# One query token against a sliding window: attention in units of two key-value pairs instead of one

## The chip, the cores and the metric

The kernel runs on one core of a Trainium2 chip. The metric is device time in microseconds for one execution. The profile of one execution shows the core's engines: TensorE (PE: matrix products into PSUM, the accumulators; PEld is its loading of weights), VectorE (DVE), ScalarE (ACT), GpSimd (POOL) and SyncE (SP), which here only issues transfers. 16 DMA engines bring data from HBM into SBUF, the on-chip memory of 128 partitions.

## What is computed

Two sequences (B = 2) decode one token each. `x` (2 x 512) is normalised to `xn`. Branch A is attention of 32 query heads over 8 key-value heads, four queries to one key-value head, over the last 4096 of 32768 cached positions. Branch B is a small gated perceptron. The end is `x + A * silu(B)`. All is float32.

```python
q = (xn @ wq).reshape(B, Sq, Hq, Dh).transpose(0, 2, 1, 3)     # 32 heads of 128
k = repeat(k_cache[:, :, Sk - W:, :], 4, axis=1)               # W = 4096
v = repeat(v_cache[:, :, Sk - W:, :], 4, axis=1)
p = softmax(einsum("bhqd,bhkd->bhqk", q, k) * Dh ** -0.5)
s = einsum("bhqk,bhkd->bhqd", p, v) ... @ wo
z = gelu(xn @ w_in); z1 = z[..., :Fh]; z2 = layernorm(z[..., Fh:])
g = silu((z1 * (w_sp * z2 + b_sp)) @ w_out)
return x + s * g
```

There are 2 x 8 = 16 pairs of a sequence and a key-value head. Each has 2 MiB of keys and 2 MiB of values to read: 64 MiB. The weights are wq (8 MiB), wo (8 MiB), w_in (3.5 MiB) and w_out (1.75 MiB).

## The kernel before

**Memory.** A pool `ring` (line 75) has four slots of 32 KB a partition. They hold, in turn, w_in, the two halves of wq, then one pair's keys and values together (`slot` in `load`, lines 114 to 120), at last the two halves of wo (lines 502 to 511). A slot is free when all that reads it is done. Position p*32 + j of a pair's window lies in partition p at place j, so that a partition reads 16 KB without a break from each cache. All large transfers are issued by SP, in the order of the program; SP waits at an issue until its slot is free, and every later issue waits behind it. `kts`, two buffers of 8 KB a partition (tag "kts" in the pool `sb`), holds transposed keys; `z`, `qs` and `qx` of the start share its buffers. `wout` has a place of its own (line 92).

**Start** (lines 87 to 322). `xn` is made and transposed. TensorE makes w_in's products `z` and transposes them (`zT_ps`), then the queries `q_ps` in four calls of `queries(k)` (lines 230 to 237), among them the perceptron's steps, then its second product `y`. The queries are copied (`qs`, ScalarE), transposed (`qx`, VectorE), spread (`xm`, `qa`) and placed by `place_queries` in `qb`, each in its own 32 columns. A few small constant matrices of zeros and ones (`sums`, `joint`, `heads`, `diag`, `selw`, `perm8`, `perm16`, lines 135 to 199) later do sums and rearrangements as matrix products.

**One pair**, functions of lines 340 to 436:

- `turn(p, q)`, q = 0 to 3: VectorE transposes a quarter of the keys (128 x 1024) in blocks of 32 x 32 into `kts`.
- `shares(p, r)`, r = 0, 1: four products of TensorE, side by side in the four column groups, multiply the queries with a quarter of the dimensions each; `keep` copies the 128 x 512 result with ScalarE and `scores` adds the four shares, with `sums` as weights. The scores of both halves of the window stand in one bank, 128 x 512.
- `row_max`, `spread_max`, `share_max`, `bias`: the maximum of each row, then over the partitions by a small product (`mo`), then the bias of the exponential.
- `probs`: ScalarE's exponential with a row sum; `probs_t`: VectorE transposes the result (128 x 512).
- `share_sum`, `weights`: the sum over partitions and its reciprocal.
- `pv(p, r)`: eight value products with 16 columns of weights and 512 values each, accumulated in `acc`; `evacuate`: four ScalarE copies scaled by the weights; `collect`: four products (`col`) bring the heads into order, and for the last pair of a set `gather` reduces them. The sets (line 327) are heads 0 to 3, 4 to 5 and 6 to 7 of both sequences.

**Order** (lines 462 to 495). One loop over the pairs, written out by hand, interleaves the turns, shares and scores of the current pair with the softmax and values of the one before and the collection of the one before that. Every engine runs its instructions in just this order (`InOrder`, line 26).

**End** (lines 525 to 570). After the last pair's softmax and values `spread` and `place` bring each set's outputs into `oT`. `wo_early` multiplies 24 of wo's 32 tiles into one bank `part`, in groups of four; the last eight, those of the third set, go into `so` together with the copied `part`. wo comes in pieces of 2, 2, 1, 1, 1, 0.5, 0.25 and 0.25 MiB, so that little is left to compute behind the last one. Two VectorE steps (`res`) apply the gate and add `x`, and SP writes 4 KB out.

Line numbers in the profile: nearly every instruction is issued by the helper of line 36, so that L36 is nearly all; the names of the tiles tell the steps apart.

Of the kernel before, what the change touches and what calls it, by code (L numbers as in the profile page):

```python
# [14 lines left out]
P = 128  # L15
# [5 lines left out]
def free_ap(t, offset, dims):  # L21

    return bass.AP(tensor=t.tensor, offset=t.offset + offset, ap=[list(t.ap[0])] + [list(d) for d in dims])

# [17 lines left out]
def kernel(  # L42
# [28 lines left out]
    SCALE = DH ** -0.5  # L71

    fit = ctx.enter_context(tc.tile_pool(name="fit", bufs=1))
# [13 lines left out]
    xs = sb.tile([B, D], F32, tag="o", name="xs")  # L87
# [4 lines left out]
    wout = cst.tile([P, FT, D], F32, tag="wout", name="wout")  # L92
# [16 lines left out]

    NP = B * HKV  # L110

    slots = {}
# [22 lines left out]
    sums = cst.tile([P, G, REP, NR, 4], F32, tag="sums", name="sums")  # L135
# [16 lines left out]
    acc = [ps.tile([P, 4, DH], F32, tag=f"acc{a}", name=f"acc{a}") for a in range(2)]  # L152
    for a in range(2):
        dve.memset(acc[a], 0.0)

# [9 lines left out]
    xn = sb.tile([B, D], F32, tag="o", name="xn")  # L165
# [9 lines left out]
    for r in range(NR):  # L175
        dve.tensor_copy(sums[:, :, :, r, 0], rowm[:, 16 * r : 16 * r + 16].rearrange("p (g i) -> p g i", g=G))
    rm = cst.tile([P, G, NR], F32, tag="rm", name="rm")
    dve.tensor_reduce(
        rm, ident.rearrange("p (g i r x) -> p g r i x", g=G, r=NR, x=4)[:, :, :, :, 0], axis=AX.X, op=ALU.add
    )  # L180
    head = cst.tile([P, REP], F32, tag="head", name="head")
    dve.tensor_reduce(head, free_ap(rowm, 0, [[8, REP], [4, NR]]), axis=AX.X, op=ALU.add)
    heads = cst.tile([P, 32, REP], F32, tag="heads", name="heads")
    dve.tensor_copy(heads, free_ap(head, 0, [[0, 32], [1, REP]]))
    joint = cst.tile([P, G, REP, NR, 4], F32, tag="joint", name="joint")
    nc.gpsimd.memset(joint, 0.0)
    for r in range(NR):
        dve.tensor_copy(joint[:, :, :, r, 0], free_ap(head, 0, [[0, G], [1, REP]]))
    diag = cst.tile([P, 4], F32, tag="diag", name="diag")
    dve.tensor_reduce(diag, free_ap(rowm, 0, [[4, 4], [1, REP]]), axis=AX.X, op=ALU.add)  # L190
    dve.tensor_reduce(selw[:, 28:32], free_ap(rowm, 0, [[1, REP], [4, 4]]), axis=AX.X, op=ALU.add)
# [12 lines left out]
    z = sb.tile([P, F], F32, tag="kts", name="z")  # L204
# [23 lines left out]
    pq = [ps.tile([P, 512], F32, tag="s", name=f"q_ps{r}", bufs=2) for r in range(NR)]  # L228
# [57 lines left out]
    qs = sb.tile([P, NR, 512], F32, tag="kts", name="qs")  # L286
    qx = sb.tile([P, NR, HC, 32], F32, tag="kts", name="qx")
# [37 lines left out]
    JH = NT // NR  # L325
# [11 lines left out]
    class Pair:  # L337
# [12 lines left out]
    def shares(p, r):  # L350
        if r == 0:
            p.sh = bank(f"sh{p.n}", 512)
        for c in range(G):
            at = 32 * (G * p.n + c) + 16 * (1 - r)
            pe.matmul(
                p.sh[32 * c : 32 * c + 32, :], qb[:, at : at + 32], p.kt[r][:, :, 32 * c : 32 * c + 32],
                start=(r == 0), stop=(r == NR - 1),
            )

    def keep(p):  # L360
        p.ss = sb.tile([P, 512], F32, tag="ss", name=f"ss{p.n}")
        act.activation(p.ss, p.sh, AF.Copy)

    def scores(p):
        p.s = ps.tile([P, 512], F32, tag="s", name=f"s{p.n}", bufs=2)
        pe.matmul(p.s, sums.rearrange("p g i r x -> p (g i r x)"), p.ss, start=True, stop=True)

    def row_max(p):
        p.m = sb.tile([P, 1], F32, tag="m", name=f"m{p.n}")
        dve.reduce_max(p.m, p.s, axis=AX.X)  # L370

    def spread_max(p):
        p.mg = sb.tile([P, G * NR], F32, tag="mg", name=f"mg{p.n}")
        dve.tensor_scalar_mul(p.mg, rm.rearrange("p g r -> p (g r)"), p.m)

    def share_max(p):
        p.mo = ps.tile([P, 512], F32, tag="mo", name=f"mo{p.n}")
        pe.matmul(p.mo[:, : G * NR], joint.rearrange("p g i r x -> p (g i r x)"), p.mg, start=True, stop=True)

    def bias(p):  # L380
        p.nb = sb.tile([P, 1], F32, tag="nb", name=f"nb{p.n}")
        dve.reduce_max(p.nb, p.mo[:, : G * NR], axis=AX.X)
        dve.tensor_scalar_mul(p.nb, p.nb, -SCALE)

    def probs(p):
        p.p = sb.tile([P, JH, 32], F32, tag="p", name=f"p{p.n}")
        p.l = sb.tile([P, 1], F32, tag="l", name=f"l{p.n}")
        act.activation(
            p.p.rearrange("p j k -> p (j k)"), p.s, AF.Exp, bias=p.nb, scale=SCALE, accum_out=p.l,
        )  # L390

    def probs_t(p):
        p.pT = sb.tile([P, JH, 32], F32, tag="pT", name=f"pT{p.n}")
        dve.transpose(p.pT.rearrange("p j h -> p (j h)"), p.p.rearrange("p j k -> p (j k)"))

    def share_sum(p):
        pe.matmul(p.mo[:, 32:33], heads.rearrange("p a h -> p (a h)"), p.l, start=True, stop=True)

    def weights(p):
        w = sb.tile([P, 1], F32, tag="w", name=f"w{p.n}")  # L400
        dve.reciprocal(w, p.mo[:, 32:33])
        p.w = sb.tile([P, 4], F32, tag="wd", name=f"wd{p.n}")
        dve.tensor_scalar_mul(p.w, diag, w)

    def pv(p, r):
        for g in range(G):
            c = JH * r + 4 * g
            pe.matmul(
                acc[p.n % 2][32 * g : 32 * g + 4 * REP].rearrange("p a d -> p (a d)"),
                free_ap(p.pT, 32 * 4 * g + 4 * r, [[8, 4 * REP]]),  # L410
                p.v[:, c : c + 4, :].rearrange("p j d -> p (j d)"), start=(r == 0), stop=(r == NR - 1),
            )

    def evacuate(p):
        p.o = sb.tile([P, 4, DH], F32, tag="o", name=f"o{p.n}")
        for jj in range(4):
            act.activation(p.o[:, jj, :], acc[p.n % 2][:, jj, :], AF.Copy, scale=p.w[:, jj : jj + 1])

    col = {}

    def collect(p):
        b, kv = divmod(p.n, HKV)
        a0, n, o1 = sets[kv]
        if a0 == 0:
            col[b] = ps.tile([P, 4, 32], F32, tag="col", name=f"col{p.n}")
        for a in range(4):
            pe.matmul(
                col[b][32 * a : 32 * a + 32], selw[:, 28 - REP * a0 : 60 - REP * a0], p.o[:, :, 32 * a : 32 * a + 32],
                start=(a0 == 0), stop=(a0 == n - 1),
            )  # L430

    def gather(p):
        b, kv = divmod(p.n, HKV)
        a0, n, o1 = sets[kv]
        if a0 == n - 1:
            dve.reduce_sum(o1[:, b, :], col[b].rearrange("p a j -> p j a"), axis=AX.X)

    def spread(i):
# [3 lines left out]
        pt = bank(f"oT_ps{i}", B, nj)  # L442
        for x in range(nx):
            pe.matmul(
                pt, perm[:, x].rearrange("p h a x -> p (h a x)"), o1[:, :, nj * x : nj * x + nj],
                start=(x == 0), stop=(x == nx - 1),
            )
        return pt

    def place(i, pt):  # L450
        dve.tensor_copy(sets[f"oT{i}"][1][:, :, 0 : 16 * B : 16], pt.rearrange("p b j -> p j b"))

    def do(f, p, *a):
        if p is not None:
            f(p, *a)

    pairs = []
    for n in range(NP):
        p = Pair()
        p.n, p.kt = n, {}  # L460
        pairs.append(p)
    AHEAD = 6
    old = prev = None
    for cur in pairs:
        if cur.n <= AHEAD:
            cur.k = load(cur.n, 0)
        if AHEAD <= cur.n < NP - 1:
            pairs[cur.n + 1].k = load(cur.n + 1, 0)
        cur.v = load(cur.n, 1)
        do(turn, cur, 0)  # L470
        if cur.n == 0:
            place_queries()
        do(row_max, prev)
        do(turn, cur, 1)
        do(shares, cur, 0)
        do(spread_max, prev)
        do(share_max, prev)
        do(collect, old)
        do(turn, cur, 2)
        do(turn, cur, 3)  # L480
        do(bias, prev)
        do(probs, prev)
        do(probs_t, prev)
        do(shares, cur, 1)
# [114 lines left out]
```

## Time and profile before

| | |
|---|---|
| median of 3 runs | 218.5 us (218.18 to 219.12) |
| the profiled execution | 219.69 us |
| its span, from the first to the last instruction | 217.6 us |
| mean granted clock of TensorE | 0.84 |
| VectorE, ScalarE busy | 123.7 us, 49.6 us |
| bytes read from HBM | 89.4 MB |

How to read the lines: a row of a group has the operation, output <- inputs with shapes, the count, then after the first bar the busy time in us and the mean ns of one, and after the second the idle time of the engine ahead of it with what ended it. One float32 product is two MATMUL instructions. In the timeline a row starts with its start and its length in us. A row of the table by stretches has the stretch, its length, the busy time of PE, PEld, DVE, ACT and POOL with the number of instructions, the granted clock of TensorE (1.00 is full), the share of DMA time and GB/s. In the 40 slices a digit is the busy share in tenths. The chain that ended last is followed back from the last instruction to what released each step.

### The profile page before, as it was taken

The numbers are of one execution on the slowest core, as the hardware profiler recorded it, in microseconds if no ns is written. First come the engines' busy times: TensorE is split into PE (matmuls) and PEld (weight loads), VectorE is DVE, ScalarE is ACT, GpSimd is POOL, SyncE is SP. The second block draws the span as 40 slices with busy tenths as digits, with TensorE's granted clock in tenths as the row PEclk, the third lists the DMA queues.
The fourth block names the chain that finished last, engine by engine and source line by source line (L and its number), as shares of the span: only waits on it lengthen the run. The fifth ranks groups of instructions, "written<-read, shape, count | busy, mean of one in ns | idle before, by whom it ended". The sixth has DMA issues, their size and how long they took to land.

```text
span 217.6 us, 2755 instructions
## 1 busy us (share of the span) xinstructions
PE 156.4 (72%) x1068; PEld 53.3 (24%) x1068; DVE 123.7 (57%) x249; ACT 49.6 (23%) x128; POOL 5.2 (2%) x19
## 2 busy tenths in 40 slices
PE   0189694946888089986898856767588856898993
PEld 0129420500222022221222211212122211225242
DVE  4511212583784677888789585866749485722001
ACT  4110211201122211433233233132222323113200
POOL 8000000000000000000000000000000000000000
PEclk9999587665599955999889999699958999558598
DMA  7999899999999999999999999999999999999970
GB/s 254 422 434 482 386 428 429 434 434 428 434 419 431 431 434 431 425 434 429 434 431 434 428 431 428 426 434 434 434 425 434 428 434 425 434 428 425 423 303 2
DMA packets 6524, 89.57 MB, mean 412 GB/s; under 512 B 734, under 2 KB 750, under 8 KB 1136
## 3 DMA queue, kind: packets, MB, share of 16 engines
q1 hardware_dynamic: 6492, 89.40, 96.4%
q8 instruction: 8, 0.13, 0.2%
q14 instruction: 4, 0.03, 0.0%
q10 hardware_dynamic: 20, 0.01, 0.0%
HBM read 89.40 MB, written 0.00 MB: 411 GB/s over the span
## 4 chain that ended last, share of the span: by engine, by line
DMA 52%; PE 28%; DVE 14%; ACT 3%; issue 1%; SPq 0%; ACTq 0%
DMA kv<-in_A_k_cache_dram 41%; DMA wq<-in_A_wq_dram 11%; DVE kts L36 11%; PE acc L36 9%; PE sh L36 6%; PE s L36 5%; PE part L36 3%; PE q_ps L36 2%; ACT ss L36 2%; DVE m L36 2%; PE oT_ps L36 1%; ACT o L36 1%; PE so L36 1%; PE col L36 1%; DVE gate L36 1%
## 5 line engine op out<-in xcount | busy, mean ns | idle before, releaser
L36 DVE STREAM_TRANSPOSE kts<-kv 128x1024 f32<-128x1024 f32 x64 | 77.2, 1227 | 16.9 <-DMA kv<-in_A_k_cache_dram 16.9
L36 PE MATMUL sh<-kts,qb 128*32 128x512 f32 x256 | 42.8, 746 | 32.6 <-DVE mg L36 24.7
L36 PE MATMUL acc<-kv,pT 128*16 128x512 f32 x256 | 36.1, 687 | 0.0
L36 ACT ACTIVATE o<-acc,wd 128x128 f32<-128x128 f32 x64 | 18.2, 367 | 60.1 <-PE acc L36 52.2
L36 PE MATMUL s<-ss,sums 128*128 128x512 f32 x32 | 22.7, 797 | 6.4 <-ACT ss L36 6.4
L36 ACT ACTIVATE p<-s,nb 128x512 f32<-128x512 f32 x16 | 11.0, 688 | 47.5 <-DVE nb L36 47.5
L36 DVE STREAM_TRANSPOSE pT<-p 128x512 f32<-128x512 f32 x16 | 11.4, 711 | 14.7 <-ACT p L36 14.7
L36 PEld LDWEIGHTS sh<-kts,qb 128*32 128x32 f32 x256 | 6.6, 121 | 51.5 <-issue 36.6
L36 PE MATMUL q_ps<-wq,xnT 128*32 128x512 f32 x64 | 10.8, 810 | 5.3 <-DMA wq<-in_A_wq_dram 5.3
L36 PEld LDWEIGHTS acc<-kv,pT 128*16 128x16 f32 x256 | 6.9, 117 | 27.6 <-issue 18.5
L36 DVE TENSOR_REDUCE m<-s 128x1 f32<-128x512 f32 x16 | 10.6, 662 | 4.3 <-PE s L36 4.3
L36 ACT ACTIVATE ss<-sh 128x512 f32<-128x512 f32 x16 | 9.6, 597 | 14.1 <-PE sh L36 12.7
L36 PEld LDWEIGHTS mo<-l,heads 128*128 128x128 f32 x32 | 5.6, 220 | 17.4 <-ACT p L36 17.4
L36 PEld LDWEIGHTS mo<-mg,joint 128*128 128x128 f32 x32 | 5.6, 219 | 16.7 <-issue 16.7
L36 PE MATMUL col<-o,selw 128*32 128x128 f32 x128 | 7.7, 319 | 1.3 <-ACT o L36 1.0
L36 PEld LDWEIGHTS s<-ss,sums 128*128 128x128 f32 x32 | 5.7, 224 | 9.4 <-ACT ss L36 6.9
L36 PE MATMUL z<-win,xnT 128*32 128x448 f32 x32 | 4.9, 752 | 3.8 <-DMA win<-in_B_w_in_dram 3.8
L36 PE MATMUL mo<-l,heads 128*128 128x1 f32 x32 | 6.9, 285 | 0.4
L36 PE MATMUL mo<-mg,joint 128*128 128x8 f32 x32 | 7.0, 293 | 0.0
L36 PE MATMUL zT_ps<-rowm,z 128*128 128x2 f32 x28 | 6.6, 370 | 0.0
L36 PEld LDWEIGHTS zT_ps<-rowm,z 128*128 128x128 f32 x28 | 6.5, 325 | 0.0
L36 PE MATMUL part<-wo,oT 128*32 128x512 f32 x48 | 6.4, 672 | 0.0
(107 smaller groups left out, 79.3 us busy)
## 6 DMA issues: line engine op xcount, KB each, us to landing
kv<-in_A_k_cache_dram SPq DMA_DIRECT2D x16, 2048.0 KB, 17.2
kv<-in_A_v_cache_dram SPq DMA_DIRECT2D x16, 2048.0 KB, 21.7
wq<-in_A_wq_dram SPq DMA_DIRECT2D x1, 4096.0 KB, 24.0
wq<-in_A_wq_dram SPq DMA_DIRECT2D x2, 2048.0 KB, 28.4
wo<-in_A_wo_dram SPq DMA_DIRECT2D x2, 2048.0 KB
win<-in_B_w_in_dram SPq DMA_DIRECT2D x1, 3584.0 KB
wo<-in_A_wo_dram SPq DMA_DIRECT2D x3, 1024.0 KB, 25.4
wout<-in_B_w_out_dram SPq DMA_DIRECT2D x1, 1792.0 KB, 14.8
```

What stands on the lines that cost most here:

```text
L36: return self.tc.keep_in_program_order(call(*args, **kwargs))
```

## The change

A **unit** is two neighbouring pairs of one sequence, interleaved over the partitions: even partitions hold the first pair, odd ones the second, each 64 consecutive positions (32 KB without a break). Keys and values of a unit are loads of 4 MiB with a ring slot each, so that 8 + 8 issues take the place of 16 + 16. The orders of the issues and of all steps are now read from a written list, `ORDER`, one word a step, with its unit and part behind the colon: K and V are the loads, T a turn, X and Y two of wo's tiles in `wo_early`.

- `turn` has 8 steps a unit, of the same size. `kts` is a pool of its own with two buffers of 16 KB; `wout`, `z`, `qs` and `qx` use these buffers too.
- `shares(p, a)` takes half of the unit's places and, for each of the two pairs i, every second column of the transposed keys; there are as many products as before. `s` has one bank for each half a; `keep`, `scores` and `row_max` are done for each half, as often as before in all.
- `spread_max`, `share_max`, `bias`, `share_sum`, `weights`, `evacuate`, `collect` are done once a unit: half as often. `other` puts a large offset into the bias of the rows of the other pair, so that their exponentials are zero.
- `probs` makes two exponentials for each half, one for each pair, and writes each to every second column of `p` (128 x 1024); `probs_t` transposes 128 x 1024. `own_sum` adds the four row sums.
- `pv` has the same number of products, with 32 columns of weights for 16. `acc` is no longer cleared at the start.
- wo is loaded by `load_wo` from the list; `wo_early` takes two tiles a step instead of four, and its steps stand among those of the last unit. The late part behind it is the same.

The lines that matter, cut:

```diff
+ORDER = """
+K:0 K:1 V:0 T:0.0 q:0 T:0.1 T:0.2 T:0.3 shares:0.0 T:0.4 T:0.5 T:0.6 keep:0.0 scores:0.0 T:0.7 shares:0.1 keep:0.1
+scores:0.1 rowmax:0.0
+K:2 V:1 T:1.0 T:1.1 T:1.2 rowmax:0.1 mg:0 shmax:0 T:1.3 silu:0 bias:0 shares:1.0 T:1.4 exp:0.0 probs_t:0.0 T:1.5 T:1.6
+exp:0.1 keep:1.0 pv:0.0 lsum:0 shsum:0 scores:1.0 T:1.7 shares:1.1 probs_t:0.1 pv:0.1 weights:0 keep:1.1 scores:1.1
+evac:0 col:0 rowmax:1.0
+K:3 V:2 T:2.0 T:2.1 T:2.2 rowmax:1.1 mg:1 shmax:1 T:2.3 bias:1 shares:2.0 T:2.4 exp:1.0 probs_t:1.0 T:2.5 T:2.6 exp:1.1
+keep:2.0 pv:1.0 lsum:1 shsum:1 scores:2.0 T:2.7 shares:2.1 probs_t:1.1 pv:1.1 weights:1 keep:2.1 scores:2.1 evac:1
+col:1 rowmax:2.0
...
+K:7 V:6 T:6.0 rowmax:5.1 T:6.1 mg:5 T:6.2 shmax:5 T:6.3 T:6.4 bias:5 exp:5.0 exp:5.1 T:6.5 shares:6.0 probs_t:5.0
+pv:5.0 lsum:5 T:6.6 keep:6.0 probs_t:5.1 T:6.7 shsum:5 scores:6.0 weights:5 shares:6.1 rowmax:6.0 pv:5.1
+V:7 T:7.0 wo:0 keep:6.1 evac:5 scores:6.1 col:5 T:7.1 T:7.2 rowmax:6.1 mg:6 shmax:6 gather:5 spread:0 T:7.3 bias:6
+T:7.4 T:7.5 shares:7.0 exp:6.0 probs_t:6.0 T:7.6 keep:7.0 pv:6.0 T:7.7 wo:1 exp:6.1 scores:7.0 shares:7.1 probs_t:6.1
+keep:7.1 lsum:6 shsum:6 scores:7.1 rowmax:7.0 weights:6 pv:6.1 evac:6 rowmax:7.1 mg:7 shmax:7 col:6 oT:0 bias:7
+gather:6 spread:1 exp:7.1 exp:7.0 probs_t:7.1 lsum:7 X:0.1 probs_t:7.0 X:0.3 X:0.2 shsum:7 weights:7 X:0.0 pv:7.0
+pv:7.1 oT:1 evac:7 X:0.7 Y:0.1 X:0.4 X:0.5 col:7 Y:0.0 X:0.6 gather:7 spread:2 oT:2 Y:0.3 Y:0.2
+"""
 
...
     ring = ctx.enter_context(tc.tile_pool(name="ring", bufs=4))
+    kts = ctx.enter_context(tc.tile_pool(name="kts", bufs=2))
...
+    wout = kts.tile([P, FT, D], F32, tag="kts", name="wout")
     sp.dma_start(wout, w_out.rearrange("(p j) d -> p j d", p=P))
     wq_v = wq.rearrange("(p k) f -> p k f", p=P)
...
-
-    def load(n, i):
-        b, kv = divmod(n, HKV)
-        if i == 0:
-            slots[n] = slot(f"kv{n}", 2, NT, DH)
-        src = (k_cache, v_cache)[i]
-        sp.dma_start(slots[n][:, i], src[b, kv, SK - W :, :].rearrange("(p j) d -> p j d", p=P))
-        return slots[n][:, i]
+    NU = NP // 2
+    UJ = 2 * NT
+
+    def load(u, src, name):
+        t = slot(f"{name}{u}", UJ, DH)
+        b, v = divmod(u, HKV // 2)
+        first = src[b, 2 * v, SK - W, :]
+        of = bass.AP(tensor=src.tensor, offset=first.offset, ap=[[UJ * DH, P // 2], [SK * DH, 2], [1, UJ * DH]])
+        sp.dma_start(t.rearrange("p j d -> p (j d)"), of)
+        return t
...
+    for i in range(2):
+        dve.tensor_copy(joint[:, :, :, i, 0], free_ap(rowm, 4 * i, [[0, G], [8, REP]]))
+    other = cst.tile([P, 2], F32, tag="other", name="other")
...
-    qs = sb.tile([P, NR, 512], F32, tag="kts", name="qs")
-    qx = sb.tile([P, NR, HC, 32], F32, tag="kts", name="qx")
+    qs = kts.tile([P, NR, 512], F32, tag="kts", name="qs")
+    qx = kts.tile([P, NR, HC, 32], F32, tag="kts", name="qx")
...
     def turn(p, q):
-        r, a = divmod(q, 2)
-        if a == 0:
-            p.kt[r] = sb.tile([P, JH, P], F32, tag="kts", name=f"kts{p.n}_{r}")
-        n = JH // 2
+        a, r = divmod(q, 4)
+        if r == 0:
+            p.kt[a] = kts.tile([P, JH, P], F32, tag="kts", name=f"kts{p.u}_{a}")
+        n = JH // 4
         dve.transpose(
-            p.kt[r][:, n * a : n * a + n].rearrange("p j d -> p (j d)"),
+            p.kt[a][:, n * r : n * r + n].rearrange("p j d -> p (j d)"),
             p.k[:, n * q : n * q + n].rearrange("p j d -> p (j d)"),
         )
...
+    def shares(p, a):
+        p.sh[a] = bank(f"sh{p.u}_{a}", 512)
+        for i in range(2):
+            for c in range(G):
+                at = 32 * (G * (2 * p.u + i) + c) + 16 * (1 - i)
+                pe.matmul(
+                    p.sh[a][32 * c : 32 * c + 32, :], qb[:, at : at + 32],
+                    free_ap(p.kt[a], 32 * c + i, [[P, JH], [2, 16]]), start=(i == 0), stop=(i == 1),
+                )
+
+    def keep(p, a):
+        p.ss[a] = sb.tile([P, 512], F32, tag="ss", name=f"ss{p.u}_{a}", bufs=1)
+        act.activation(p.ss[a], p.sh[a], AF.Copy)
+
+    def scores(p, a):
+        p.s[a] = ps.tile([P, 512], F32, tag=f"s{a}", name=f"s{p.u}_{a}")
+        pe.matmul(p.s[a], sums.rearrange("p g h i x -> p (g h i x)"), p.ss[a], start=True, stop=True)
...
+    def bias(p):
+        nb = sb.tile([P, 1], F32, tag="nb", name=f"nb{p.u}")
+        dve.reduce_max(nb, p.mo[:, : G * 4], axis=AX.X)
+        p.nb = sb.tile([P, 2], F32, tag="nb2", name=f"nb2_{p.u}")
+        dve.tensor_scalar(p.nb, other, nb, -SCALE, op0=ALU.add, op1=ALU.mult)
+        p.l = sb.tile([P, 2, 2], F32, tag="l", name=f"l{p.u}")
+
+    def probs(p, a):
+        p.p[a] = sb.tile([P, JH, 32], F32, tag="p", name=f"p{p.u}_{a}")
+        for i in range(2):
+            act.activation(
+                free_ap(p.p[a], i, [[2, 512]]), p.s[a], AF.Exp, bias=p.nb[:, i : i + 1], scale=SCALE,
+                accum_out=p.l[:, a, i : i + 1],
+            )
+
+    def probs_t(p, a):
+        p.pT[a] = sb.tile([P, JH, 32], F32, tag="pT", name=f"pT{p.u}_{a}")
+        dve.transpose(p.pT[a].rearrange("p j c -> p (j c)"), p.p[a].rearrange("p j k -> p (j k)"))
...
+    def pv(p, a):
+        if a == 0:
+            p.acc = ps.tile([P, 4, DH], F32, tag="acc", name=f"acc{p.u}", bufs=2)
+        for n in range(JH // 4):
+            g, c = n % G, JH * a + 4 * n
             pe.matmul(
-                p.sh[32 * c : 32 * c + 32, :], qb[:, at : at + 32], p.kt[r][:, :, 32 * c : 32 * c + 32],
-                start=(r == 0), stop=(r == NR - 1),
+                p.acc[32 * g : 32 * g + 32].rearrange("p a d -> p (a d)"),
+                free_ap(p.pT[a], 32 * 4 * n, [[4, 32]]), p.v[:, c : c + 4, :].rearrange("p j d -> p (j d)"),
+                start=(a == 0 and n < G), stop=(a == 1 and n >= JH // 4 - G),
             )
...
+    def load_wo(n):
+        t = slot(f"wo{n}", 16, D)
         a = 0
-        for i in of:
-            nj = SETS[i][2]
+        for i in ((0,), (1, 2))[n]:
             for j, n in (((0, 8), (8, 8)), ((0, 4), (4, 4)), ((0, 4), (4, 2), (6, 1), (7, 1)))[i]:
                 sp.dma_start(t[:, a : a + n, :], wo_s[i][:, j : j + n, :])
                 blocks.append((t[:, a : a + n, :], sets[f"oT{i}"][1], j))
                 a += n
+
     EARLY = 24
...
-    def wo_early(n, a0=0):
+    def wo_early(n, at):
         nonlocal done
+        if done == 0:
+            part.append(ps.tile([P, 512], F32, tag="s0", name="part"))
         t, oT, j = blocks[n]
-        for a in range(a0, a0 + 4):
+        for a in range(at, at + 2):
             g = done % G
             pe.matmul(
-                part[32 * g : 32 * g + 32, :], oT[:, j + a, :], t[:, a, :], start=(done < G), stop=(done >= EARLY - G)
+                part[0][32 * g : 32 * g + 32, :], oT[:, j + a, :], t[:, a, :], start=(done < G), stop=(done >= EARLY - G)
             )
             done += 1
 
...
+    for line in ORDER.strip().split("\n"):
+        for name in line.split():
+            name, at = name.split(":")
+            u, _, a = at.partition(".")
+            step(name, int(u), (int(a),) if a else ())
```

More of the change, by code (lines that the diff above doesn't have):

```diff
@@ L227 @@
     assert HKV == NR * G
-    pq = [ps.tile([P, 512], F32, tag="s", name=f"q_ps{r}", bufs=2) for r in range(NR)]
+    pq = [ps.tile([P, 512], F32, tag=f"s{r}", name=f"q_ps{r}") for r in range(NR)]
     def queries(k):
@@ L396, in share_sum @@
[L396 to L411, printed above, removed]
+    def shares(p, a):
+        p.sh[a] = bank(f"sh{p.u}_{a}", 512)
+        for i in range(2):
+            for c in range(G):
[4 more added lines that the diff above has]
+                )
@@ L545 @@
-    place(2, spread(2))
-    wo_early(0, 4)
-    wo_early(2)
-    wo_early(1, 0)
-    wo_early(1, 4)
-    wo_early(3)
-    parts = sb.tile([P, D], F32, tag="o", name="parts")
-    act.activation(parts, part, AF.Copy)
+    part = []
+    STEPS = dict(
+        T=turn, rowmax=row_max, mg=spread_max, shmax=share_max, bias=bias, exp=probs, probs_t=probs_t, lsum=own_sum,
+        shsum=share_sum, weights=weights, shares=shares, keep=keep, scores=scores, pv=pv, evac=evacuate, col=collect,
+        gather=gather,
+    )
```

233 lines of the change are left out of this document (97 added, 136 removed).

## The prediction

> **What bounds the kernel now.** First the top of the page and its 40 slices.
>
> ```profile
> span 217.6 us, 2755 instructions
> ...
> PE 156.4 (72%) x1068; PEld 53.3 (24%) x1068; DVE 123.7 (57%) x249; ACT 49.6 (23%) x128; POOL 5.2 (2%) x19
> ...
> DMA  7999899999999999999999999999999999999970
> GB/s 254 422 434 482 386 428 429 434 434 428 434 419 431 431 434 431 425 434 429 434 431 434 428 431 428 426 434 434 434 425 434 428 434 425 434 428 425 423 303 2
> ```
>
> No engine is busy for more than 72% of the span, while the DMA digits stand at 9 nearly everywhere up to the 38th slice. A slice is 217.6 / 40 = 5.44 us; the last two move 303 and 2 GB/s, so something goes on after the transfers. The table by stretches gives the rate and the end of the transfers (last two columns: DMA share, GB/s):
>
> ```profile
> 16.00:34.00 18.00, 15.32 (x90) 8.83 (x82) 3.56 (x18) 3.65 (x6) 0.00 (x0) 0.81 0.99 424
> 40.00:190.00 150.00, 110.65 (x742) 32.59 (x734) 107.87 (x179) 37.65 (x104) 0.00 (x0) 0.85 1.01 430
> 200.00:210.00 10.00, 9.59 (x66) 3.28 (x70) 1.06 (x6) 1.14 (x4) 0.00 (x0) 0.70 1.00 418
> 211.40:211.60 0.20, 0.20 (x8) 0.08 (x4) 0.00 (x0) 0.00 (x0) 0.00 (x0) 1.00 0.25 92
> ```
>
> 430 GB/s for 150 us, whatever the engines do, and the last bytes move at about 211.6. The kernel is a row of transfers with a tail of computing behind it. I read the tail in the timeline: TensorE's rows, VectorE's end, and the issues of the last two pieces of wo with their time to landing.
>
> ```profile
> 199.81 0.56 PE L36 MATMUL mo<-l,heads 128*128 128x1 f32 x2
> 200.30 3.62 PE L36 MATMUL acc<-kv,pT 128*16 128x512 f32 x16
> 203.70 1.93 PE L36 MATMUL part<-wo,oT 128*32 128x512 f32 x8
> 205.40 0.65 PE L36 MATMUL col<-o,selw 128*32 128x128 f32 x8
> 206.47 1.07 PE L36 MATMUL oT_ps<-o,perm 128*128 128x16 f32 x8 [0.41 <-DVE o L36]
> 207.46 4.50 PE L36 MATMUL part<-wo,oT 128*32 128x512 f32 x40
> 211.78 1.06 PE L36 MATMUL so<-wo,oT 128*32 128x128 f32 x32
> 212.74 0.43 PE L36 MATMUL so<-parts,rowm 128*32 128x128 f32 x8
> 212.98 1.06 PE L36 MATMUL so<-wo,oT 128*32 128x128 f32 x32
> ```
> ```profile
> 214.10 0.29 DVE L36 TENSOR_TENSOR res<-so,gate 128x128 f32<-128x128 f32 x1 [6.28 <-PE so L36]
> ```
> ```profile
> 187.59 5.17 SPq L36 DMA_DIRECT2D wo<-in_A_wo_dram  x2
> ```
> ```profile
> wo<-in_A_wo_dram SPq DMA_DIRECT2D x2, 256.0 KB, 23.8
> ```
>
> The first lands 23.8 us after 187.59, at 211.4; the second, issued long before that, stands behind it in the same queue: 0.26 MB / 430 GB/s = 0.6 us later, 212.0. TensorE, though, ends the `part` products at 211.96 and the `so` products at 214.04, with no wait for a transfer beside these rows. From there 217.6 - 214.04 = 3.56 us lead to the end (two VectorE steps and the output transfer). After the last landing only 8 `so` instructions are unavoidable, 1.06 us x 8 / 32 = 0.27. **The least that today's transfers allow is 212.0 + 0.27 + 3.56 = 215.8 us of span, 1.8 below 217.6.** What shortens neither the transfers nor this tail brings nothing.
>
> **The change, part by part.** *Work of a unit (two pairs)*, from the groups:
>
> ```profile
> L36 DVE STREAM_TRANSPOSE kts<-kv 128x1024 f32<-128x1024 f32 x64 | 77.2, 1227 | 16.9 <-DMA kv<-in_A_k_cache_dram 16.9
> L36 PE MATMUL sh<-kts,qb 128*32 128x512 f32 x256 | 42.8, 746 | 32.6 <-DVE mg L36 24.7
> L36 PE MATMUL acc<-kv,pT 128*16 128x512 f32 x256 | 36.1, 687 | 0.0
> L36 ACT ACTIVATE o<-acc,wd 128x128 f32<-128x128 f32 x64 | 18.2, 367 | 60.1 <-PE acc L36 52.2
> L36 PE MATMUL s<-ss,sums 128*128 128x512 f32 x32 | 22.7, 797 | 6.4 <-ACT ss L36 6.4
> L36 ACT ACTIVATE p<-s,nb 128x512 f32<-128x512 f32 x16 | 11.0, 688 | 47.5 <-DVE nb L36 47.5
> L36 DVE STREAM_TRANSPOSE pT<-p 128x512 f32<-128x512 f32 x16 | 11.4, 711 | 14.7 <-ACT p L36 14.7
> ```
>
> TensorE keeps its share products, value products (32 columns of weights for 16, the same instructions streaming 512) and score products: (42.8 + 36.1 + 22.7) / 8 = 12.7 us a unit. Collections and the two small products halve. VectorE keeps the 64 key transposes; `probs_t` becomes 16 of 128x1024, a key transpose's shape: 16 x 1.227 = 19.6 us, so with the keys (77.2 + 19.6) / 8 = 12.1 us a unit, and some 2 for the small steps, which halve. ScalarE makes each exponential twice, 11.0 us more in all, and saves half of 18.2. The unit's 8 MiB take 8.39 MB / 430 GB/s = 19.5 us, which hides all of it with 5 us to spare; I cost it at nothing in the middle. The stride of two in the share operand and in the written probabilities is in no row. Between nothing and a doubling of the shares (42.8 / 8 = 5.4 us a unit) the transfers still cover it; I take nothing, since `acc` reads its weights at a stride of eight today and is no slower than `sh`.
>
> *Start.* `wout`, `z`, `qs` and `qx` now share two buffers, so `qs` waits for the `y` products. Today's rows:
>
> ```profile
> 40.06 2.78 PE L36 MATMUL y<-wout,hT 128*32 128x128 f32 x56
> 40.35 0.33 SPq L36 DMA_DIRECT2D kv<-in_A_k_cache_dram  x1
> ...
> 60.83 1.25 DVE L36 STREAM_TRANSPOSE kts<-kv 128x1024 f32<-128x1024 f32 x1 [0.42 <-DMA kv<-in_A_k_cache_dram]
> ```
>
> `y` ends at 42.84. SP's queue becomes K0 K1 V0 K2 V1 K3 V2 ..., 4 MiB each. K2 takes wq's slot, free at 40.35 as now, and with it 29.25 MiB are out. The key load that lands at 60.83 is the end of 23.25 MiB, so the queue lasts to 60.8 + 6.29 MB / 430 = 75.4. V1 waits for K0's last turn: 42.84, some 5 us for qs, qx, xm and the queries, eight turns of 1.2: about 58. K3 waits for K1's last turn, behind one more unit of VectorE's 14 us with the silu and some waiting: 74 to 77; V1 has stretched the queue to 85. Eight us of cover, so nothing; if it were gone, each further us of delay would come out of the transfers.
>
> *32 KB pieces.* The 16 KB pieces of 32 issues become 32 KB pieces of 16. wq's first load has 32 KB pieces already (2 x 4096 floats a partition). Two rows time it, the first from the timeline, the second a link of the chain that ended last:
>
> ```profile
> 11.90 0.97 PE L36 MATMUL z<-win,xnT 128*32 128x448 f32 x4 [3.84 <-DMA win<-in_B_w_in_dram]
> ```
> ```profile
> 1.64 24.03 DMA wq<-in_A_wq_dram
> ```
>
> From win's landing (11.9) to wq's (1.64 + 24.03 = 25.67) wout and wq moved, 6.03 MB in 13.8 us: 437 GB/s. But the stretch 16 to 34, half of it the same load, has 424. For the 67.1 MB of keys and values (156.0 us at 430) that is 2.4 us less or 2.3 us more. I take 0.7 less: the first is the nearer, landing to landing, but a single pair of times, and the other speaks against it. [...]
>
> *The tail.* Behind V7 lie 8 MiB of wo, as now behind the last value load; counted back from 212.0, 8.39 MB / 430 = 19.5: V7 lands at 192.5, the first half of `wo0` 4.9 later at 197.3, each 0.7 earlier with the gain. V6 lands one load earlier, at 182.7. Behind it TensorE has values 6.0, scores, shares 7.1, the sum, scores, values 6.1, at full clock 1.9 + 1.1 + 1.9 + 0.4 + 1.1 + 1.9 = 8.3 us, with half a us of ScalarE's copy between: 191.5. Evacuation 1.2, four exponentials with their sums at 0.9 and the second `probs_t` 1.2: 197.5. At half clock it comes some 3 us later. TensorE's list from there: X0.1 X0.3 X0.2, the sum, X0.0, values of unit 7, four X/Y steps (beside the evacuation), collect, two steps, spread, two steps, `so`. **X0.1 waits for wo at 197.3, and the value products, ready or nearly so, are queued behind it**; evacuation, collection and spread wait for these. Prices at full clock: a step of 4 instructions 0.43 (4.50 for 40, less 0.2 of start), values 3.85 (two of `acc` x16, each half of the 3.62 above), collect 0.42, spread 1.07, `so` 2.08 (211.96 to 214.04). At half clock a step is 0.86, the values 7.2, the sum 0.56. So the clock decides (column PEclk):
>
> ```profile
> 36.60:42.00 5.40, 5.36 (x56) 2.58 (x59) 1.70 (x3) 1.19 (x2) 0.00 (x0) 0.50 1.01 434
> 42.20:44.00 1.80, 1.72 (x23) 0.67 (x14) 1.37 (x3) 0.28 (x1) 0.00 (x0) 0.99 1.02 437
> 202.60:206.00 3.40, 3.40 (x24) 0.73 (x16) 0.00 (x0) 1.14 (x4) 0.00 (x0) 0.50 1.03 434
> 206.00:209.00 3.00, 2.59 (x28) 1.51 (x28) 0.48 (x2) 0.00 (x0) 0.00 (x0) 0.98 0.97 406
> ```
>
> After an idle stretch it is 0.50 from 36.6 and back at 42.2, 5.6 us after dense products began; and 0.50 up to 206, back behind. In the new tail TensorE has little but tiny products from about 193 on, so I let it start at half, and come back after 5.6 us. With the gain: start 196.6, back at 202.2. Three steps 199.2, sum 199.7, X0.0 200.6, values 1.6 us at half (0.8 of 3.85) and 3.0 at full 205.2, four steps 206.9, collect 207.3, two steps 208.2, spread 209.3, two steps 210.1, `so` 212.2. The landing would allow 212.0 - 0.7 + 0.27 = 211.6, so TensorE is late. Saved: 214.04 - 212.2 = 1.8.
>
> The sum: the middle 0, the start 0, pieces and tail together -1.8. Against the profiled execution (219.69 us, span 217.6, 2.09 around it) that gives 217.9. That execution lies 1.2 above the median of 218.5; the same 1.8 taken off the median gives **216.7**.
>
> [...]
>
> **The rivals.**
>
> *Floor:* the clock isn't lost, or returns early, and `so` ends with the last landing. For it: the spread of unit 6 and collect run shortly before. Then `so` ends at 211.6 with my 0.7 and at 209.9 with 2.4 (2.4 to 4.2 saved); with 1.1 it is 215.7.
>
> [...]
>
> *The tail at half clock*, the one on the other side. If it returns only at 211: values 208.5, four steps 211.5, collect 211.9, then 212.7, 213.8, 214.7, `so` 216.8: 2.7 lost, 221.2. It decides from a return about 10 us after X0.1, where 1.1 us are lost. Against it: both rows above come back sooner.
>
> *Rows from two pairs, 16 MB apart, read more slowly.* At 418, the slowest wide row above, 67.1 MB take 160.5 us, 4.5 more; less the 1.8 of the tail: 221.2. Against it: keys and values, two arrays, alternate in the queue today at 430.
>
> **How the numbers follow.** Forecast 0.36, floor 0.17, no gain 0.27, half clock 0.12, slow rows 0.08. A measurement tells 0.5% (1.1 us) from no change: faster is forecast and floor, 0.53; same 0.27; slower 0.20. The range runs from the floor with half of its further gain, 215.0, to a half clock that returns a little after its point, 220.0. The forecast alone: 216.0 to 217.4.
>
> **What would show it.** Right: 430 GB/s or a little more from 40 to 190; no SP wait that empties the queue; V7's products not before `part`; PEclk 0.5 at the first X step; `so` near 212. Wrong: a GB/s digit that sags in the middle (slow rows) or near 75 to 90 (the start's cover gone); `so` waiting for DMA (floor); PEclk 0.5 through `col` (half clock).

## The result, and the profile after

| | before | after |
|---|---|---|
| median, runs beside each other | 218.55 us (218.18 to 220.62, 20 runs) | 218.03 us (217.10 to 218.67, 20 runs) |
| ratio of the times | | 0.9961 [0.9943, 0.9979] |
| profiled execution, its span | 219.69, 217.6 us | 217.48, 215.7 us |

The changed kernel is 0.4% faster by the ratio, which lies at that of the two means (217.96 and 218.81 us); by the medians it is 0.5 us, or 0.24%. The forecast was 1.8 us. The page of the changed kernel, in the same lines as that of before:

```profile
span 215.7 us, 2477 instructions
...
PE 143.5 (67%) x972; PEld 51.6 (24%) x972; DVE 126.3 (59%) x217; ACT 50.9 (24%) x128; POOL 5.2 (2%) x19
...
DMA  6999999999999999999999999999999999999990
GB/s 256 426 438 444 407 428 468 395 463 407 462 413 441 431 425 444 419 448 407 456 413 456 419 441 431 419 444 422 450 409 462 407 450 419 441 401 428 419 376 23
DMA packets 4219, 89.56 MB, mean 415 GB/s; under 512 B 478, under 2 KB 494, under 8 KB 880
```

The picture is the same: transfers at 9 in all slices but the ends, no other engine over 67%. There are 4219 packets; the page of before has this line:

```profile
DMA packets 6524, 89.57 MB, mean 412 GB/s; under 512 B 734, under 2 KB 750, under 8 KB 1136
```

The table by stretches (columns as before) gives the rate and the tail's clock:

```profile
40.00:190.00 150.00, 101.12 (x645) 31.49 (x641) 110.92 (x149) 37.44 (x99) 0.00 (x0) 0.81 1.00 432
194.50:197.00 2.50, 0.12 (x2) 0.02 (x2) 2.13 (x3) 0.93 (x4) 0.00 (x0) 0.99 1.00 426
197.00:200.00 3.00, 2.97 (x12) 0.65 (x12) 0.00 (x0) 0.00 (x0) 0.00 (x0) 0.50 0.98 418
200.00:200.50 0.50, 0.50 (x2) 0.00 (x0) 0.00 (x0) 0.00 (x0) 0.00 (x0) 0.61 1.08 459
200.50:205.00 4.50, 4.50 (x44) 2.09 (x46) 0.48 (x3) 0.00 (x0) 0.00 (x0) 1.00 1.00 421
```

432 GB/s from 40 to 190 where before had 430. TensorE does next to nothing from 194.5 to 197.0 (0.12 us), then works at a granted 0.50 until 200.4 (the half microsecond with 0.61 is 0.39 us at 0.50 and 0.11 at 1.00), and at 1.00 behind it: 3.4 us after the first X step began. Last the timeline, first the two late issues of the start, then the tail:

```profile
56.70 0.54 SPq L65 DMA_DIRECT2D v<-in_A_v_cache_dram  x1
74.12 0.54 SPq L65 DMA_DIRECT2D k<-in_A_k_cache_dram  x1
...
197.03 3.56 PE L65 MATMUL part<-wo,oT 128*32 128x512 f32 x12 [2.41 <-DMA wo<-in_A_wo_dram]
...
209.92 1.06 PE L65 MATMUL so<-wo,oT 128*32 128x128 f32 x32
...
211.12 1.06 PE L65 MATMUL so<-wo,oT 128*32 128x128 f32 x32
212.24 0.29 DVE L65 TENSOR_TENSOR res<-so,gate 128x128 f32<-128x128 f32 x1 [2.85 <-PE so L65]
```

In this one execution the forecast is met at its ends: the first X step starts at 197.03 (forecast 196.6), at half clock, `so` ends at 212.18 (212.2), and the span is 215.7 (217.6 - 1.8 = 215.8). Between them two errors cancel, which is luck: the full clock is back 1.8 us earlier than forecast (200.4 for 202.2), and the first three X steps take 3.56 us for the 2.58 that the forecast gave them. Against the profiled execution of before, 1.9 us of span are gone, and 2.2 us of time, since 1.78 us lie outside the span here and 2.09 there. The medians differ by 0.5. So the question is not what the change did in that pair of profiles, but why the pair doesn't stand for the rest.

### The profile page after: what moved, and what is told of

Read it like the earlier page. It is cut to its first block, busy times and chain, and to the rows that moved or that the text cites. A ratio compares the mean times of both kernels' runs of the same rounds, so it can differ in the third digit from the quotient of the medians.

```text
span 215.7 us, 2477 instructions
## 1 busy us (share of the span) xinstructions
PE 143.5 (67%) x972; PEld 51.6 (24%) x972; DVE 126.3 (59%) x217; ACT 50.9 (24%) x128; POOL 5.2 (2%) x19
## 2 busy tenths in 40 slices
DMA packets 4219, 89.56 MB, mean 415 GB/s; under 512 B 478, under 2 KB 494, under 8 KB 880
## 4 chain that ended last, share of the span: by engine, by line
DMA 57%; PE 20%; DVE 17%; ACT 4%; issue 1%; ACTq 0%
DMA k<-in_A_k_cache_dram 40%; DMA wo<-in_A_wo_dram 12%; DVE kts L65 11%; PE acc L65 7%; DMA win<-in_B_w_in_dram 5%; PE sh L65 5%; PE part L65 4%; ACT p L65 3%; PE s L65 3%; DVE pT L65 2%; DVE m L65 1%; PE so L65 1%; DVE gate L65 1%; DVE nb L65 1%; ACT ss L65 1%
## 5 line engine op out<-in xcount | busy, mean ns | idle before, releaser
L65 DVE STREAM_TRANSPOSE kts<-k 128x1024 f32<-128x1024 f32 x64 | 75.7, 1219 | 25.7 <-DMA k<-in_A_k_cache_dram 25.7
L65 PE MATMUL acc<-v,pT 128*32 128x512 f32 x256 | 36.4, 676 | 6.9 <-DVE pT L65 4.0
L65 ACT ACTIVATE p<-s,nb 128x512 f32<-128x512 f32 x32 | 22.5, 730 | 38.6 <-DVE nb L65 38.6
L65 DVE STREAM_TRANSPOSE pT<-p 128x1024 f32<-128x1024 f32 x16 | 19.6, 1226 | 2.5 <-ACT p L65 2.5
L65 PE MATMUL s<-ss,sums 128*128 128x512 f32 x32 | 18.8, 671 | 2.1 <-ACT ss L65 2.1
L65 PE MATMUL mo<-mg,joint 128*128 128x16 f32 x16 | 4.2, 338 | 23.6 <-DVE mg L65 23.6
L65 PEld LDWEIGHTS acc<-v,pT 128*32 128x32 f32 x256 | 11.4, 143 | 32.6 <-issue 21.8
L65 ACT ACTIVATE o<-acc,wd 128x128 f32<-128x128 f32 x32 | 9.1, 367 | 19.5 <-PE acc L65 19.5
L65 PE MATMUL part<-wo,oT 128*32 128x512 f32 x48 | 9.5, 709 | 2.4 <-DMA wo<-in_A_wo_dram 2.4
L65 ACT ACTIVATION_READ_ACCUMULATOR p<-s,nb 128x1 f32 x32 | 6.4, 200 | 0.0
```

Of the source, the lines that this page charges most:

```text
L65: return self.tc.keep_in_program_order(call(*args, **kwargs))
```

## The experiments

My theory has two parts. **A**: what is gained is time of the transfers, and it goes with the size of a piece. **C**: before's tail ends with the last landing already in most executions, so that an earlier tail brings nothing there, and the changed kernel's own tail is late where the last unit meets TensorE at half clock. The main rival is the prediction's own reason, that some 1.1 us come from a tail that ends earlier in every execution; the expectations name further ones, each with its words. **E**, for the last runs: the transfers' gain goes with the number of issues. Each ratio is to the kernel before, run beside the kernel on the same chip.

**The changed kernel again**, the yardstick, twice.

> The changed kernel once more, as the yardstick for the runs beside it. Both theories: about 0.996 of the kernel before. Its profile shows a second tail: with TensorE's clock coming back at another time, the so products end between 211.6 and 213.5.

> The changed kernel once more, as the yardstick of the runs beside it on the same chip. All theories: 0.996 to 0.997 of the kernel before, 217.9 to 218.2 us.

218.13 us (217.34 to 219.18), 0.9966 [0.9938, 0.9994]; and 217.98 (217.24 to 218.90), 0.9977 [0.9956, 0.9998]. The profiled executions of these two took 218.66 and 218.90, over a microsecond more than the first one; their spans are 216.6 and 216.3 for 215.7, and the rest lies outside the span (2.06 and 2.60 us for 1.78). Where the span grew, the timeline and the table by stretches show; the first:

```profile
196.78 3.63 PE L65 MATMUL part<-wo,oT 128*32 128x512 f32 x12 [2.79 <-DMA wo<-in_A_wo_dram]
...
212.03 1.06 PE L65 MATMUL so<-wo,oT 128*32 128x128 f32 x32
```
```profile
202.00:202.50 0.50, 0.50 (x4) 0.00 (x0) 0.00 (x0) 0.00 (x0) 0.00 (x0) 0.50 1.05 442
202.50:203.00 0.50, 0.50 (x8) 0.19 (x4) 0.00 (x0) 0.00 (x0) 0.00 (x0) 0.82 1.01 426
```

The second:

```profile
196.69 3.63 PE L65 MATMUL part<-wo,oT 128*32 128x512 f32 x12 [2.55 <-DMA wo<-in_A_wo_dram]
...
211.78 1.06 PE L65 MATMUL so<-wo,oT 128*32 128x128 f32 x32
```
```profile
202.00:202.50 0.50, 0.50 (x8) 0.13 (x4) 0.00 (x0) 0.00 (x0) 0.00 (x0) 0.73 0.97 410
```

X0.1 starts as early as in the first profile, even 0.2 to 0.3 us earlier: the transfers are the same. But the full clock is back only at 202.7 and 202.3 (0.82 and 0.73, taken apart as above), 5.9 and 5.6 us after X0.1 where it was 3.4 in the first, and `so` ends at 213.09 and 212.84 for 212.18. The prediction had taken 5.6 for the clock, and 212.2 for the end of `so`: with the clock as forecast, its tail was 0.6 us too short (212.84). So in three executions of one kernel the full clock came back 3.4, 5.9 and 5.6 us after X0.1.

**16 KB pieces in the changed kernel.** The same loads, each issued in two halves of every partition's run (shortened here, as the diffs below are).

```diff
-        sp.dma_start(t.rearrange("p j d -> p (j d)"), of)
+        for h in range(2):   # places h * NT to h * NT + NT of each partition
+            sp.dma_start(t[:, h * NT : h * NT + NT, :]..., part_of)
```

> The changed kernel with every key and value load issued as two, so that a partition reads 16 KB pieces again; order, tail and units stay. Theory A (the gain is in the transfers, the tail was close to the last landing in most executions of both kernels): the gain goes, ratio 0.999 to 1.002, and 40 to 190 us move 430 GB/s. Theory B (the gain is the tail): it stays, 0.995 to 0.997, at whatever rate.

218.82 us (218.28 to 219.48), 1.0003 [0.9981, 1.0024]: the whole gain is gone, 0.69 us over the changed kernel beside it (218.13), and by the medians it is 0.35 us slower than before (218.47). That is what A says; a gain from the tail's new order should have stayed. The rate from 40 to 190 us, also named in the expectation, decides nothing: 431 GB/s here, 431 and 432 in the changed kernel.

**Two issues for one, with 32 KB pieces.** The same number of issues as in the last kernel, but one for each pair, on every second partition.

```diff
-        sp.dma_start(t.rearrange("p j d -> p (j d)"), of)
+        for i in range(2):
+            sp.dma_start(t[i : P : 2].rearrange("p j d -> p (j d)"), of)   # of: pair i alone
```

> The changed kernel with 32 issues of keys and values, as before the change, but pieces of 32 KB, as after it: each load is issued twice, once for each pair, on every second partition. It parts the number of issues from the size of a piece. Theory A (the gain is the time of the transfers and goes with the size of a piece): as the changed kernel, 0.996 to 0.997 of the kernel before, about 218.1 us. Rival E (it goes with the number of issues, 16 for 32): as the changed kernel with 16 KB pieces, 1.000, about 218.8 us. A third way: a transfer on every second partition is spread less evenly over the DMA engines and comes out slower than both, over 219.

217.89 us (217.29 to 218.57), 0.9961 [0.9938, 0.9984], as the changed kernel beside it (217.98): A, and E falls, as does the third way (over 219).

**8 KB pieces**, four issues a load, written as the 16 KB ones.

> The changed kernel with pieces of 8 KB, each load issued four times: 64 issues and 8192 pieces, where the changed kernel has 16 and 2048, and the one with 16 KB pieces 32 and 4096. The step from 32 to 16 KB cost 0.69 us for 2048 more pieces. Theory A with a fixed cost for each piece: 4096 more pieces cost twice that, 1.4 us more than with 16 KB, about 220.2 us, 1.007 of the kernel before. If the cost of a piece is hidden in part, or the 0.69 us had another source: 218.8, as with 16 KB. Rival E (issues) also gives 1.4 us more here; the run with 32 issues of 32 KB pieces tells it from A.

219.76 us (219.45 to 220.58), 1.0062 [1.0043, 1.0081], 1.78 over the changed kernel beside it. A's 1.007 lies within the interval, though its 1.4 us over the 16 KB kernel came out as 1.1 by the gaps to the changed kernel (1.78 - 0.69).

These three are best compared where X0.1 starts, since it waits for the first half of `wo0`, which stands behind all keys and values in the queue. The lines are from the timelines of the 16 KB kernel, the one by pairs and the 8 KB kernel, each with the packets of its page:

```profile
197.75 3.63 PE L65 MATMUL part<-wo,oT 128*32 128x512 f32 x12 [7.48 <-DMA wo<-in_A_wo_dram]
...
211.95 1.06 PE L65 MATMUL so<-wo,oT 128*32 128x128 f32 x32
```
```profile
DMA packets 6523, 89.56 MB, mean 414 GB/s; under 512 B 734, under 2 KB 750, under 8 KB 1136
```
```profile
196.89 3.17 PE L65 MATMUL part<-wo,oT 128*32 128x512 f32 x12 [2.02 <-DMA wo<-in_A_wo_dram]
```
```profile
DMA packets 4476, 89.56 MB, mean 416 GB/s; under 512 B 735, under 2 KB 751, under 8 KB 1137
```
```profile
198.79 3.63 PE L65 MATMUL part<-wo,oT 128*32 128x512 f32 x12 [8.46 <-DMA wo<-in_A_wo_dram]
```
```profile
DMA packets 11132, 89.57 MB, mean 412 GB/s; under 512 B 1246, under 2 KB 1262, under 8 KB 1648
```

With 32 KB pieces the wait ends at 196.69 to 197.03 in the three profiles of the changed kernel and at 196.89 with two issues; with 16 KB at 197.75, 0.9 later than the mean of the three (196.83); with 8 KB at 198.79, 1.0 later still. The first step adds 2048 pieces, the second 4096, so the cost for one is not shown to be constant: 0.9 for the first 2048 and 1.0 for the next 4096, from one execution each, with 0.3 us between executions of the same kernel. The 0.69 us are no colder tail, as far as single profiles show: from X0.1 to the end of `so` the 16 KB kernel takes 213.01 - 197.75 = 15.26 us, the changed one 15.15 and, in the two later profiles, 16.31 and 16.15. The 257 small packets that 16 more issues bring (4476 against 4219) cost nothing that can be seen.

**Fewer early tiles of wo**, in before and in the changed kernel: 4 for 24, to take the tail's work away and lay the transfers bare.

```diff
-    EARLY = 24
+    EARLY = 4
-    wo_early(0, 4)   # and four more calls; in the changed kernel ten X and Y steps
```

> The kernel before with 20 of the 24 early tiles of wo left out of the products (all of wo is still loaded), so that TensorE is done long before the last landing and the end is what the transfers allow. Theory A: 0.3 to 0.8 us below the kernel before, ratio 0.996 to 0.999. Theory B: 1 to 2 us below, 0.991 to 0.995. The rule of the prediction (least span 215.8 against a typical span of about 216.7) says 0.9 us.

> The same cut in the changed kernel (20 of 24 early tiles left out of the products). Theory A: 0.5 us or more below the cut kernel before, since the transfers themselves are shorter, and no more than 0.3 us below the changed kernel. Theory B: equal to the cut kernel before within 0.2 us, and 0.3 to 1 us below the changed kernel.

Before: 219.56 us (219.02 to 220.83), 1.0037 [1.0013, 1.0062], slower with less to do. The changed kernel: 218.24 (217.78 to 218.81), 0.9971 [0.9946, 0.9997]. No theory had expected the first. The timeline and the stretches of before, cut:

```profile
209.95 1.94 PE L36 MATMUL so<-wo,oT 128*32 128x128 f32 x32 [8.24 <-DMA wo<-in_A_wo_dram]
...
212.05 1.33 PE L36 MATMUL so<-wo,oT 128*32 128x128 f32 x32
```
```profile
203.00:209.00 6.00, 0.00 (x0) 0.00 (x0) 0.00 (x0) 0.00 (x0) 0.00 (x0) 0.50 1.00 421
```

TensorE waits 8.24 us for wo and has nothing else; the clock falls to 0.50, and `so`'s first 32 instructions take 1.94 us where they took 1.06. So the run gives no clean floor: what the cut took from the tail it gave back as a cold `so`. The changed kernel, cut, has the same cold `so`:

```profile
209.12 1.94 PE L65 MATMUL so<-wo,oT 128*32 128x128 f32 x32 [1.72 <-DMA wo<-in_A_wo_dram]
```

Its `so` starts 0.83 us earlier and ends 0.66 earlier (212.72 for 213.38). The medians stand 1.3 apart, of which 1.0 is span (216.45 for 217.45) and 0.3 lies outside it. That speaks for A again (0.7 to 1.0 us), though the two kernels' lists differ in more than the pieces.

**Before, profiled twice more.**

> The kernel before, unchanged, for a second profile. Theory C (the tail term was mis-sized since the one profile of before shows a late tail: half clock from 199 to 206): here TensorE's clock falls at other times, the so products end between 212.5 and 213.5, span about 216.5, time about 218.5. Rival D (the tail is always so late and the profiled execution is just slower than the timed ones): so ends at 214.0 again, span 217.5.

> The kernel before, unchanged, a third profile. Theory C: another end of the so products, between 212.3 (the last landing allows no less) and 214.1. Rival D: 214.0.

218.24 and 219.82 us, the same kernel; the second alone is what rival D expected. The first one's stretches and its last products:

```profile
190.00:195.00 5.00, 3.78 (x26) 1.30 (x22) 1.90 (x8) 1.55 (x5) 0.00 (x0) 1.00 1.02 436
203.00:209.00 6.00, 5.59 (x56) 2.16 (x48) 0.48 (x2) 0.00 (x0) 0.00 (x0) 0.95 1.01 422
```
```profile
209.74 1.08 PE L36 MATMUL so<-wo,oT 128*32 128x128 f32 x32 [0.43 <-DMA wo<-in_A_wo_dram]
...
212.17 0.42 PE L36 MATMUL so<-wo,oT 128*32 128x128 f32 x8 [0.20 <-DMA wo<-in_A_wo_dram]
```

The second one's:

```profile
190.00:195.00 5.00, 4.74 (x16) 1.33 (x16) 1.99 (x6) 0.60 (x1) 0.00 (x0) 0.50 1.02 433
199.50:206.00 6.50, 6.50 (x37) 2.15 (x37) 0.58 (x4) 1.14 (x4) 0.00 (x0) 0.50 0.99 420
```
```profile
213.10 1.06 PE L36 MATMUL so<-wo,oT 128*32 128x128 f32 x32
```

The second is the execution from which the prediction was made, over again: half clock through 190 to 195, half clock up to 206, `so` ending at 214.16 with no wait for a transfer. In the first the clock is full from 190 to 195 and back before 206, the tail arrives earlier, and **`so` waits for wo**, at its start and again at its last eight instructions: it ends at 212.59, with the landing. In that execution an earlier tail would win nothing, and D falls. Of the 113 runs of before in all comparisons here 87 lie at 219 us or below, with a median of 218.39, and 26 above, with a median of 219.78. The first of the two stands with the 87, the second and the profile of the prediction with the 26. For 93 of the 113 the span is on record too: 60 have one of 216.0 to 216.4 us, where the first has 216.1 and ends with the landing. That is the first half of C, and the rival, a tail that brings 1.1 us in every execution, falls.

**A warm TensorE.** Products that nobody reads, 128 x 512 each, fill the idle time ahead of the tail: one behind the last `share_max` and two behind `spread:1` in the changed kernel, one behind the last `share_max` in before.

```diff
+    def warm(n):
+        t = bank(f"warm{n}", 512)
+        for i in range(n):
+            pe.matmul(t, sums..., qb[:, 512 * i : 512 * i + 512], start=True, stop=True)
-... shmax:7 col:6 oT:0 bias:7 gather:6 spread:1 exp:7.1 ...
+... shmax:7 W:1 col:6 oT:0 bias:7 gather:6 spread:1 W:2 exp:7.1 ...
```

> The changed kernel with three more products of TensorE in the idle stretches of its tail (128x128 weights, 512 columns, into a free bank, read by nobody): one behind the last share_max, two behind the second spread. If the clock at the first X step sets how late the tail is (theory C), PEclk is near 1.0 from 195 to 200, so ends at 211.6 to 211.9 and the median falls by 0.4 to 0.8 us against the changed kernel, to 0.992 to 0.995 of the kernel before. If the tail is bound by landings already, nothing: 0.996. If the products come too late and only delay X, slower by up to 1 us.

> The kernel before with one such product in TensorE's idle stretch ahead of the last collect. Theory C: the half clock behind 199 becomes rare and the median falls by 0 to 0.5 us, 0.9975 to 1.0; the slow ones near 219 to 220.6 disappear. Rival D: 1.5 us faster, 0.993.

The changed kernel, warm: 217.40 us (217.14 to 218.22), 0.9937 [0.9915, 0.9959]. Before, warm: 218.64 (218.30 to 220.06), 0.9998 [0.9973, 1.0023], no gain; its late executions did not disappear, as C had expected, with 3 of 12 above 219 us for 5 of the 23 of before. The changed kernel's stretches and end:

```profile
195.00:200.00 5.00, 4.27 (x25) 1.38 (x28) 1.95 (x6) 0.27 (x2) 0.00 (x0) 1.00 0.98 418
200.00:205.00 5.00, 4.39 (x44) 1.66 (x40) 0.00 (x0) 1.14 (x4) 0.00 (x0) 1.00 1.02 426
```
```profile
197.00 1.91 PE L65 MATMUL part<-wo,oT 128*32 128x512 f32 x12 [0.73 <-DMA wo<-in_A_wo_dram]
...
211.62 0.42 PE L65 MATMUL so<-wo,oT 128*32 128x128 f32 x8 [0.17 <-DMA wo<-in_A_wo_dram]
```

Full clock in both stretches, the twelve instructions of the first three X steps take 1.91 us for 3.56 in the first profile, and now `so` waits for wo here too and ends at 212.04. Three rows of before, warm:

```profile
196.94 1.10 PE L36 MATMUL warm<-qb,sums 128*128 128x512 f32 x2
...
200.10 1.92 PE L36 MATMUL acc<-kv,pT 128*16 128x512 f32 x16
...
212.29 0.43 PE L36 MATMUL so<-wo,oT 128*32 128x128 f32 x8 [0.21 <-DMA wo<-in_A_wo_dram]
```

The last instructions wait for the same landing as in the first profile above. This execution ran at half clock from 190 to 195 as the second one did, but behind the product that nobody reads its value products take 1.92 us, where the prediction's rows have 3.62 at half clock: in this execution the product probably kept the tail from being late, which one profile does not show, and by the 3 of 12 it does not do so in every one. With both tails at the landing, the landings can be compared: 212.17 and 212.29 for before, 211.62 for the changed kernel.

> The changed kernel with the three products that nobody reads (one behind the last share_max, two behind the spread of the second set), once more, beside the changed kernel on the same chip. Theory C (the changed kernel ends late in those executions in which the last unit meets TensorE at half clock; with the products it ends at the last landing in all): 0.5 to 0.8 us below the changed kernel, 0.992 to 0.995 of the kernel before, with the narrower spread of the two. If the 0.7 us of the first such run came from its chip or its hour: as the changed kernel, 0.996 to 0.997.

Once more, beside the changed kernel: 217.30 us (217.10 to 218.28), 0.9946 [0.9929, 0.9964], 0.68 under the 217.98 of the changed kernel there. In time the spread is hardly narrower, because three of the 24 warm runs lie 2.7 to 2.8 us outside their span; but all 24 spans are 215.3 to 215.7 us, where the 44 of the changed kernel are 215.3 to 216.9. That is the second half of C. Its last products:

```profile
211.48 0.42 PE L65 MATMUL so<-wo,oT 128*32 128x128 f32 x8 [0.21 <-DMA wo<-in_A_wo_dram]
```

The mean of the two warm ends (211.55) is 0.68 us before that of the two of before (212.23).

## Why the prediction was wrong, and where it was right

- **The bound** was right: transfers, with a tail behind. The floor was drawn 0.3 us too low: the last eight instructions of `so` end at 212.59, not at 212.27, because the last landing lets them start at 212.17, not 212.0, and they take 0.42 for 0.27. Before's least span on record is 216.0, where the floor was 215.8.
- **The middle and the start at nothing**: right. V:1 went out at 56.70 (about 58) and K:3 at 74.12 (74 to 77), and no DMA digit sags behind them.
- **The pieces, 0.7 us**: right, the exact size by luck, since it was picked between rows that gave 2.4 gained (2.5 by its own rates) and 2.3 lost. 0.68 between the last landings, 0.69 between the medians with 32 and 16 KB pieces, 0.9 at X0.1.
- **The tail, 1.1 us: this step failed.** "That execution lies 1.2 above the median of 218.5; the same 1.8 taken off the median gives 216.7." In most executions of before the tail has no 1.1 us to give: it ends with the landing, `so` at 212.59 in the first later profile where the prediction's had 214.04. The prediction's profile showed one of the other 26 in 113. The text held the contradiction already: 216.7 less the 2.09 around the span is 214.6, but its own floor, with the 0.7 gained, was a span of 211.6 + 3.56 = 215.2, or 217.3 us in time. The forecast for the median lay below its own floor. The warm kernel's 217.30 and 217.40 lie on that floor, but by two errors that cancel: the span's floor was 0.3 too low (215.5), and the time around the span fell by 0.3.
- **The new tail's own length** was mis-sized too: 3.56 to 3.63 us for the first three X steps at half clock, for 2.58. The price of a step was read from ten steps in a row (4.50 us); three alone take 1.91 at full clock in the warm kernel, for 1.29. Why is not shown.
- **The clock in the new tail** was right, and it is what the median still pays: X0.1 at 196.7 to 197.0 on a TensorE idle for 2.4 to 2.8 us, full clock back 3.4 to 5.9 us later (taken: 5.6). Against the warm kernel it costs 0.68 us in the median (217.98 to 217.30). The forecast had this cost, but inside a tail that still gained.
- **Around the span** the forecast kept 2.09 us. All 93 runs of before have 2.05 to 2.18; the 44 of the changed kernel have a median of 1.81, the widest 3.48. So some 0.3 us of the gain lies outside the span, a term at which the prediction did not look; no run here shows its cause.
- **The sum as the runs have it**: from before to the warm kernel 1.19 and 1.03 us (218.59 to 217.40, 218.33 to 217.30). 0.7 of it are the landing and 0.3 the time outside the span; the rest, up to 0.2, fits before's late executions, which lift its median by 0.4 at most (218.46, the median of all 113, less the lowest, 218.09). From the warm kernel back to the changed one 0.7 are lost. That leaves 0.3 to 0.5 of gain; 0.34 to 0.52 were measured.
- **The rivals.** The floor was the nearest of them in mechanism: it is where the changed kernel goes once the clock is held, with `so` at 212.04 and 211.90 for 211.6. No gain (0.27) is, by the prediction's own bound of 1.1 us, where the 0.5 us between the medians fall; that the pieces bring nothing is refuted all the same, by the 16 KB run (0.69 us). The tail at half clock to 211 was in no profile (its sum starts X0.1 at 197.3, without the 0.7 of the pieces, and is some 0.4 too long for that). Slow rows are refuted: 432 GB/s.

Open: why one execution of before works at half clock from 190 to 195 and another, with the same instructions, at full. No run shows it, nor why the clock came back 3.4 us after X0.1 in one execution of the changed kernel and 5.9 in another. Open too are the cause of the 0.3 us outside the span and whether the cost for each piece is constant.

## What to carry to other kernels

A profile is one execution. Where its time stands above the median, find out what it lost before a saving is taken from it, and hold the forecast for the median against the floor drawn from the profile: a forecast below that floor counts something twice. When a kernel is bound by transfers, look at TensorE's idle time ahead of the tail: three products that nobody reads were worth more here (0.7 us) than the change, which regrouped every step of the attention (0.5 us).

## What the runs showed of the hardware

- Less work made the kernel slower: leaving 20 of wo's 24 early tiles out of before cost 0.4% (1.0037), since TensorE then waited 8.24 us and began `so` at half clock (0.50 granted; 1.94 us for its first 32 instructions, for 1.06).
- TensorE can stay at half clock though it is listed as busy: 4.74 of 5.00 us from 190 to 195 and 6.50 of 6.50 from 199.5 to 206 in the second of the two later profiles of before, with 0.50 granted in both. What releases it is not shown.
- Pieces of 32 KB a partition were faster than pieces of 16 KB: X0.1 started at 196.83 on average against 197.75, 0.6% of the 156 us that the 67.1 MB of keys and values take at 430 GB/s.
